# Linear attention and a max-out FFN on one core: first and last chunk by halves, one exponential over two PSUM banks, a new order

## Chip, cores, metric

The kernel runs on one core of one Trainium2 chip. The metric is the device time of one execution in microseconds; the kernel before took 294.62 us (median of three runs).

## What is computed

```python
def phi(x):                                   # x: q or k, (8, 8, 576, 64)
    proj = einsum('bhsd,df->bhsf', x, w_phi)  # 128 features
    proj = proj - max(abs(proj), axis=-1)
    return concatenate([exp(proj), exp(-proj)], axis=-1)
q_p, k_p = phi(q), phi(k)
kv  = einsum('bhsf,bhsd->bhfd', k_p, v);  z = sum(k_p, axis=2)
num = einsum('bhsf,bhfd->bhsd', q_p, kv); den = einsum('bhsf,bhf->bhs', q_p, z) + 1e-06
x   = (num / den) as (8 * 576, 512)           # 4608 tokens
h   = maximum(maximum(x @ w1, x @ w2), x @ w3)   # w1, w2, w3: 512 x 768
out = h @ w_out                               # 768 x 512
```

## The kernel before

Attention goes in 16 units: a unit is half a batch, four heads of 576 tokens. The 512 first tokens of each head are 16 tiles of 128 (four a head), the 64 tokens left of each two heads share a tile, so a unit has 18 tiles. `HU`, `MT` and `UT` are 4, 16 and 18.

The steps of a unit, by their names in the code: loads of q, k and v (`L`, `Lt` for the 64 tokens at the end of each head, `Lv`); for the units 0 to 3 q and k are loaded and cast by POOL's queue and transposed on PE (`T`, line 495) and copied (`Tc`), for the others they are cast (`C`, line 510) and transposed by a DMA. Then the projections of tokens on the rows (`G`, line 536) into `psq` and `psk`, the exponentials `ek` (line 545) and the absolute maxima `rk` and `rq` (line 548). The maxima of k scale v (`va`, line 566), and `K` (line 587) adds up kv and z. A second product, of transposed q (`M`, line 607), gives the features on the rows: `psm`, whose exponentials `eq` (line 613) go to `Eq`. `N` (line 638) multiplies them with kv for each of the two signs; `xu` scales the one by exp of minus twice the maximum (`sq`), `xw` adds the other, `xr` takes the reciprocal of the denominator and `x` (line 648) divides. The result is turned into `xT`: on PE for the units below `X_PE` = 6 (line 658, copied at 661), by a DMA transpose for the others (line 665).

The FFN goes in nine chunks: chunk b takes the 512 first tokens of each head of batch b, the last chunk the 8 x 64 tokens left over (`c_i == B`). The maximum with w1 is taken out of the products: w2 - w1 and w3 - w1 (`wd`, line 763) go through a product each (`up`, `up2`, line 688), are cut at zero and maximised (`t1`, line 696 or 698; `h`, line 694), and x @ (w1 @ w_out) is added to the down product (lines 716 and 721). The products `wt` and `wm` (lines 775 and 789) make w1 @ w_out once. `osb` (line 729) copies a result out of PSUM, `store` writes it.

The weights are loaded by four DMAs of POOL's queue (line 421).

The order of the work is written out by hand: the string `PLAN` lists every step once, with the step's number, the engine (T is PE, D DVE, A ACT, G POOL, S the SP queue), the buffer slots that it takes, and a due time. Each engine runs its steps in the order of the list and waits for what a step needs; the due time sets nothing else but where idle products could be put between, and there are none. PSUM's eight banks are slots as well. `4G0@0.4` is step 4 on POOL with slot 0.

The start of the list, with what the steps are: 4 and 5 load unit 0's q, 6 and 8 its k, 2 loads w_phi, 10 the ends of q (`Lt`), 11 v, 93 and 92 unit 1's k and q, 253 and 252 unit 3's, 177 and 176 unit 2's, 12 and 96 cast the ends of q for the units 0 and 1 (line 487), 1173 to 1176 load the weights:

```
4G0@0.4 6S0@0.4 2S@1.0 0G@1.2 5G@1.8 8S@2.2 93G1@2.7 10S0@2.8 92G@3.5 7D@3.7 11S0@4.1 3D@4.2 13T0@4.3 253G2@4.3
14D0@5.0 252G@5.2 9A@5.3 24T001200@5.8 19T34@6.0 27D@6.3 21A@6.5 12G@6.6 15T5@6.7 96G@6.8 23D@6.9 26A@7.0 17T6@7.2
178S0@7.2 16D@7.5 20A@7.5 177G0@7.5 25A@8.0 18D@8.1 29T70@8.2 22D@8.3 176G@8.4 39T35@8.5 63T6200@8.6 30A@8.7 28D@8.9
65A@9.2 1173G@9.2 94D@9.5 42D@9.6 34T41@9.7 31A@9.7 95S@9.8 33D@10.0 1176G@10.0 41A@10.2 36A@10.5 43D@10.6 101T7@10.7
```

13, 15 and 17 are unit 0's transposes on PE (17 those of the tail), 24, 19, 29, 34 and 39 its projections.

Of the kernel before, what the change touches and what calls it, by code (L numbers as in the profile page):

```python
# [19 lines left out]
P = 128  # L20
# [5 lines left out]
HU = 4  # L26
# [10 lines left out]
EARLY = 2  # L37
WARM = 28.0
# [8 lines left out]
class Buf:  # L47


    def __init__(self, pool, make):  # L50
        self.pool, self.make = pool, make
        self.users, self.tile, self.index, self.left, self.free = [], None, None, 0, 0.0
        self.locked = 0.0
# [31 lines left out]
4G0@0.4 6S0@0.4 2S@1.0 0G@1.2 5G@1.8 8S@2.2 93G1@2.7 10S0@2.8 92G@3.5 7D@3.7 11S0@4.1 3D@4.2 13T0@4.3 253G2@4.3  # L85
14D0@5.0 252G@5.2 9A@5.3 24T001200@5.8 19T34@6.0 27D@6.3 21A@6.5 12G@6.6 15T5@6.7 96G@6.8 23D@6.9 26A@7.0 17T6@7.2
178S0@7.2 16D@7.5 20A@7.5 177G0@7.5 25A@8.0 18D@8.1 29T70@8.2 22D@8.3 176G@8.4 39T35@8.5 63T6200@8.6 30A@8.7 28D@8.9
65A@9.2 1173G@9.2 94D@9.5 42D@9.6 34T41@9.7 31A@9.7 95S@9.8 33D@10.0 1176G@10.0 41A@10.2 36A@10.5 43D@10.6 101T7@10.7
1174G@10.8 32D@10.9 40A@10.9 99T3@11.1 64A@11.2 97T5@11.5 102D1@11.5 1175G@11.6 67A@11.7 37D@11.7 68T0@12.1 58T67@12.2
401S0@12.2 44A0@12.2 98D@12.3 66A@12.4 46G0@12.5 69A@12.9 100D@13.0 108T112511@13.1 35A@13.2 38D@13.6 62A@13.6  # L90
113T31@13.8 256G@13.9 181G@14.1 70A@14.1 112D@14.2 45G@14.3 48A@14.4 103T40@14.6 109A@14.6 117D@14.8 257T2@14.9
104A@15.1 111D@15.4 261T3@15.6 61A@15.6 329S0@15.6 47G@15.7 49G@15.9 262D2@16.0 105A@16.1 107D@16.2 52T073@16.4
59A@16.5 106D@16.8 110A@17.0 50G@17.2 116D@17.4 60A@17.5 118T45@17.7 259T0@18.0 53A@18.0 122D@18.1 128A1@18.2
114A@18.4 123T67@18.5 51G@18.6 121D@18.7 400S@18.8 130G1@18.8 54A@18.9 152T411@18.9 115A@19.1 126D@19.4 154A@19.6
127D@19.7 55T31@19.7 124A@19.9 260D@20.0 119A@20.1 129G@20.1 182T6@20.4 56A@20.6 258D@20.7 125A@20.8 186T0@20.9
71A0@21.1 147T37@21.3 187D0@21.3 132A@21.3 57D@21.5 153A@21.5 72T20@21.6 135G@21.7 183D@21.7 120A@21.8 131G@21.9
75T14@22.0 133G@22.2 149A@22.3 73D0@22.3 184T5@22.4 76D@22.8 155A1@22.8 328S@22.9 151A@23.0 136T162@23.0 74D@23.2
148A@23.4 134G@23.5 77D@23.6 83T10@23.7 150A@23.9 138D@24.0 142T34@24.2 185D@24.2 137A@24.4 80T27@24.6 145A@24.6
78D0@24.8 139T65@25.0 84D1@25.1 143A@25.1 79G0@25.2 81D@25.5 146A@25.6 1187T1@25.7 85D@25.9 327S@26.0 144A@26.1
1185T2@26.3 82D@26.3 1188A0@26.6 406G1@26.6 141D@26.7 159T40@26.9 140D@27.0 86D1@27.2 156T37@27.2 160D0@27.5  # L100
1186A@27.5 87G@27.5 1183T5@27.6 157D@27.9 164T61@28.2 161D@28.3 1184A@28.5 223T4300@28.6 158D@28.7 88T2@28.9 404G@29.0
165D1@29.2 90T0@29.2 225A@29.4 403G@29.5 179D1@29.6 167T75@29.6 166D@29.7 1195T6@29.9 89A@29.9 405G@30.1 254D@30.1
168D@30.2 227A@30.5 162D0@30.7 334G2@30.7 91D@30.9 255S@31.0 224A@31.0 1189T21@31.2 163D1@31.4 226A@31.5 1196A@32.0
169D@32.1 1D@32.5 206T007000@32.6 197T4365@32.7 170D1@32.7 1190A@32.8 209D@33.0 172T1@33.3 171D@33.3 208A@33.5
1191T2@33.6 207A@33.9 201D@34.0 198A@34.2 180S@34.2 1179G@34.6 210D@34.7 199A@34.8 174T0@34.9 205D@35.0 1193T4@35.2
203A@35.3 200D@35.6 175A@35.8 173D@36.2 1192A@36.4 188T7630@36.6 1178G@36.7 1194A@36.9 228T1@37.0 1207T2@37.2
195D@37.3 230A@37.4 189A@37.7 196D@37.9 1209T4@38.1 229A@38.2 1208A1@38.4 204D@38.5 407G@38.8 1205T1@39.0 191D@39.1
202A@39.3 1177G@39.5 408S1@39.6 1181D@39.7 194A@39.7 1203T3@39.9 1210A@40.2 192D@40.3 1215T2@40.7 211A0@40.7
# [184 lines left out]
def kernel(  # L293
# [95 lines left out]
    def side(t):  # L389
        return int(t >= MT // 2)  # L390
# [465 lines left out]
```

## Time and profile before

| | |
|---|---|
| three runs | 292.95, 296.05, 294.62 us; median 294.62 |
| the profiled execution | 292.23 us, of which the span from the first to the last instruction is 290.1 |
| mean granted TensorE clock | 0.994 |
| busy share of the span | PE 93%, PEld 52%, DVE 79%, ACT 71%, POOL 54% |
| chain that ended last | PE 74%, DMA 15%, DVE 6% |
| DMA | 49.92 MB in 70662 packets |

The profile's rows name a line, an engine, an operation and its tiles (written <- read), and give the start, the busy time, and in brackets the idle time just before with what ended it. Matmul records overlap in a pipeline, so PE's busy time holds short waits too. `POOLq` and `SPq` are rows of the engines' queues, which issue DMAs.

### The profile page before, as it was taken

The numbers are of one execution on the slowest core, as the hardware profiler recorded it, in microseconds if no ns is written. First come the engines' busy times: TensorE is split into PE (matmuls) and PEld (weight loads), VectorE is DVE, ScalarE is ACT, GpSimd is POOL, SyncE is SP. The second block draws the span as 40 slices with busy tenths as digits, with TensorE's granted clock in tenths as the row PEclk, the third lists the DMA queues.
The fourth block names the chain that finished last, engine by engine and source line by source line (L and its number), as shares of the span: only waits on it lengthen the run. The fifth ranks groups of instructions, "written<-read, shape, count | busy, mean of one in ns | idle before, by whom it ended". The sixth has DMA issues, their size and how long they took to land.

```text
span 290.1 us, 8572 instructions
## 1 busy us (share of the span) xinstructions
PE 270.6 (93%) x3502; PEld 151.3 (52%) x3502; DVE 230.2 (79%) x458; ACT 204.7 (71%) x493; POOL 157.7 (54%) x163
## 2 busy tenths in 40 slices
PE   1589997899999999998999999999999999999994
PEld 1367643456546645663565445655465555444442
DVE  2699886989998889998999988999999785264430
ACT  2699985789998899689864899999969681210001
POOL 7397659557678636576866396660758533100000
PEclk9998999999999999999999999999999999999999
DMA  7999998793897962799987899627084212100065
GB/s 141 226 280 215 262 259 198 207 273 119 299 279 158 244 192 46 182 321 282 254 245 198 209 333 206 127 21 217 5 129 139 90 37 62 66 3 2 0 217 145
DMA packets 70662, 49.92 MB, mean 172 GB/s; under 512 B 47072, under 2 KB 58720, under 8 KB 70624
## 3 DMA queue, kind: packets, MB, share of 16 engines
q1 hardware_dynamic: 65232, 44.25, 58.7%
q0 software_dynamic: 5312, 5.08, 10.7%
q8 instruction: 27, 0.44, 0.6%
q14 instruction: 11, 0.09, 0.1%
q10 hardware_dynamic: 80, 0.07, 0.1%
HBM read 34.67 MB, written 9.44 MB: 152 GB/s over the span
## 4 chain that ended last, share of the span: by engine, by line
PE 74%; DMA 15%; DVE 6%; issue 1%; POOL 1%; SPq 1%; DVEq 0%; POOLq 0%
PE ups L688 31%; PE ops L721 14%; DMA w_bf<-in_moe_w_dram 11%; PE ops L716 10%; PE psn L638 6%; PE kvps L587 5%; PE psq L536 4%; PE psm L607 3%; DMA q_raw<-in_q_dram 2%; DMA xT<-x_sb 2%; DVE w_bf L763 1%; DVE x_sb L648 1%; DVE y L644 1%; PE pxT L658 1%; PE psk L536 1%
## 5 line engine op out<-in xcount | busy, mean ns | idle before, releaser
L688 PE MATMUL ups<-xT,w_bf 128*128 128x512 bf16 x432 | 99.5, 379 | 4.2 <-DVE w_bf L763 1.4
L545 ACT ACTIVATE Ek<-psk 128x512 bf16<-128x512 f32 (+1 forms) x160 | 83.6, 572 | 12.9 <-PE psk L536 6.7
L566 POOL TENSOR_TENSOR vab<-v_raw,em 128x1152 bf16<-128x1152 f32 (+1 forms) x36 | 69.5, 1950 | 35.8 <-ACT em L558 35.8
L613 ACT ACTIVATE Eq<-psm 128x512 bf16<-128x512 f32 (+1 forms) x160 | 81.9, 588 | 3.1 <-PE psm L607 1.9
L688 PEld LDWEIGHTS <-w_bf 128*128 128x128 bf16 x432 | 39.9, 98 | 52.6 <-issue 4.4
L548 DVE TENSOR_REDUCE mk<-psk 128x4 f32<-128x512 f32 (+1 forms) x80 | 48.7, 630 | 4.7 <-PE psk L536 3.2
L721 PE MATMUL ops<-wout_bf,hT 128*128 128x512 bf16 (+1 forms) x222 | 51.7, 373 | 0.0
L548 DVE TENSOR_REDUCE mq<-psq 128x4 f32<-128x512 f32 (+1 forms) x80 | 48.6, 628 | 2.3 <-PE psk L536 1.3
L696 ACT ACTIVATE hT<-ups 128x512 bf16<-128x512 f32 x36 | 21.8, 611 | 29.0 <-PE ups L688 28.8
L694 DVE TENSOR_TENSOR hT<-hT,ups 128x512 bf16<-128x512 bf16 x54 | 35.2, 678 | 8.3 <-PE ups L688 7.5
L648 POOL TENSOR_TENSOR x_sb<-y,rden 128x640 bf16<-128x640 f32 x22 | 27.4, 1253 | 21.9 <-DVE rden L646 21.0
L641 DVE TENSOR_TENSOR y<-psn,sq 128x325 f32<-128x325 f32 x64 | 29.5, 488 | 6.9 <-PE psn L638 5.0
L721 PEld LDWEIGHTS <-hT 128*128 128x128 bf16 x222 | 20.5, 98 | 21.9 <-issue 0.5
L644 DVE TENSOR_TENSOR y<-y,psn 128x325 f32<-128x325 f32 x64 | 29.4, 488 | 1.4
L638 PEld LDWEIGHTS <-Eq 128*128 128x128 bf16 x640 | 25.0, 97 | 10.3 <-issue 2.5
L729 ACT COPY osb<-ops 128x512 f32<-128x512 f32 (+1 forms) x23 | 13.2, 583 | 23.0 <-PE ops L721 22.7
L638 PE MATMUL psn<-kv_sb,Eq 128*128 128x65 bf16 x640 | 27.5, 194 | 1.3 <-issue 0.4
L536 PE MATMUL psq<-wph,qkT 64*128 64x128 bf16 x288 | 25.9, 224 | 1.2 <-DVE qkT L500 1.0
L536 PEld LDWEIGHTS <-qkT 64*128 64x128 bf16 x576 | 18.6, 97 | 15.8 <-issue 12.0
L536 PE MATMUL psk<-wph,qkT 64*128 64x128 bf16 x288 | 25.4, 224 | 0.3 <-DVE v_raw L479 0.3
L716 PE MATMUL ops<-xT 128*128 128x512 bf16 x96 | 24.6, 380 | 0.0
L587 PE MATMUL kvps<-vab,Ek 64*128 64x65 bf16 x1152 | 22.7, 193 | 0.3 <-ACT Eq L613 0.2
(58 smaller groups left out, 259.9 us busy)
## 6 DMA issues: line engine op xcount, KB each, us to landing
v_raw<-in_v_dram SPq DMA_DIRECT2D x16, 576.0 KB, 7.2
out_dram<-osb SPq DMA_DIRECT2D x32, 256.0 KB, 3.4
k_raw<-in_k_dram SPq DMA_DIRECT2D x12, 576.0 KB, 5.4
q_raw<-in_q_dram SPq DMA_DIRECT2D x12, 512.0 KB, 5.5
w_bf<-in_moe_w_dram POOLq DMA_DIRECT2D x3, 768.0 KB, 25.1
q_raw<-in_q_dram SPq DMA_DIRECT2D x16, 64.0 KB, 5.5
qk_bf<-in_k_dram POOLq DMA_DIRECT2D x3, 288.0 KB, 7.3
qk_bf<-in_q_dram POOLq DMA_DIRECT2D x3, 256.0 KB, 9.9
```

What stands on the lines that cost most here:

```text
L536: nc.tensor.matmul(ps()[:, i, :], lhsT=cols[r0:r0 + D, :], rhs=wph[r0:r0 + D, :], start=True, stop=True)
L545: "ek", {"ACT": 0.485 if n == 4 else 0.28}, lambda s=s, t0=t0, n=n, psk=psk: nc.scalar.activation(Ek[s]()[:, t0:t0 + n, :], psk()[:, 0:n, ...
L548: reds.append(nd(kind, {"DVE": 0.607 if n == 4 else 0.34}, lambda ps=ps, m=m, t0=t0, n=n: nc.vector.tensor_reduce(m()[:, t0:t0 + n], ps()[ ...
L566: made.append(any_of(n_, lambda n_, g=g, t0=t0, t1=t1: (nc.vector if n_.eng == "DVE" else nc.gpsimd).tensor_tensor(vab()[:, g, t0:t1, 0:D] ...
L587: nc.tensor.matmul(kvps[ab]()[:, pr, g, :], lhsT=Ek[g]()[r, t, :], rhs=vab()[r, g, t, :], start=(pr == prs[0] and g + j == 0), stop=(pr == ...
L613: "eq", {"ACT": 0.485 if n == 4 else 0.28}, lambda s=s, t0=t0, n=n, psm=psm: nc.scalar.activation(Eq[s]()[:, t0 * P:(t0 + n) * P], psm()[: ...
L638: nc.tensor.matmul(psn[g]()[:, c, :], lhsT=Eq[g]()[:, t0:t0 + P], rhs=kv()[:, pr, ab, g, :], start=True, stop=True)
L644: sums.append(nd("xw", {"DVE": 0.42}, lambda ab=ab, psn=psn, y=y: nc.vector.tensor_tensor(y()[:, ab], y()[:, ab], psn[1](), ALU.add), [n_] ...
L688: nc.tensor.matmul(ups(), lhsT=w_bf[i + 1][:, ct, j * P:(j + 1) * P], rhs=tokens_of(ct), start=(ct == 0), stop=(ct == CT - 1))
L694: nc.vector.tensor_tensor(hT()[:, j, :], hT()[:, j, :], ups(), ALU.max)
L716: nc.tensor.matmul(ops_()[:, 0:width], lhsT=tile_of(ct, tt), rhs=line_w[c_i > MOVE][:, ct, cols], start=(ct == 0), stop=False)
L721: nc.tensor.matmul(ops_()[:, 0:width], lhsT=hT()[:, j, tt * P:(tt + 1) * P], rhs=wout_bf[:, j, cols], start=False, stop=(j == JT - 1))
```

## The change

- A unit's q tiles are put in another order (`tile_of_q`): first the two first tiles of each of the four heads, then the two second ones. So the product `M` and the exponentials of one step give the first 256 tokens of all four heads, and `N`, `xu`, `xw`, `xr`, `x` and the turning of x go by halves of the tokens (2 tiles, then 3 with the shared tile) where they went by pairs of heads.
- The two `M` products of a step write one tile of two PSUM banks, and one exponential of 1024 columns reads it, where there were two of 512.
- `xu` can run on ACT, as one small multiplication for each head and tile; 26 of the 64 do.
- The units 14 and 15 turn x on PE, as the first six do. For the units 0, 1, 14 and 15 the reciprocal is taken for each pair of heads.
- The chunks 0 and 7 go as two of 256 tokens each, the last one as 384 and 128.
- PSUM is one tile of eight banks, of which each buffer is a slice.
- Unit 0's second transposes need both loads of k; q's casts of the units 4 to 15 are in two pieces each.
- The list is rewritten as a whole. Its start, where 1155 to 1158 are the weights now, 251 and 250 load unit 3's k and q, and the steps 0 to 43 are what they were:

```
8S0@0.7 5G0@1.2 6S@1.3 2S@1.9 4G@2.1 92G1@2.9 10S0@3.1 0G@3.8 9A@3.9 93G@4.3 11S0@4.4 176G2@5.2 7D@5.4 3D@5.9 177G@6.0
15T0@6.0 13T1@6.7 16D0@6.7 1155G@6.8 14D@7.4 29T000200@7.5 1158G@7.7 34T34@7.7 30A@8.0 33D@8.0 24T15@8.1 19T67@8.4
36A@8.4 1156G@8.4 32D@8.6 20A@8.9 38D@9.2 1157G@9.2 35A@9.4 23D@9.8 21A@9.9 12G@10.1 25A@10.4 37D@10.4 17T0@10.4
251G0@10.8 31A@10.9 18D@11.0 28D@11.2 26A@11.3 64T000@11.4 58T2@11.5 96G@11.7 39T46@11.7 65A@11.8 22D@11.8 59A@12.1
```

The last of unit 3's loads is `250G@29.9`; its transposes stand at 41.2 to 43.6, among the products of chunk 0, where the list before had them at 14.9 to 18.0.

The core of the diff, without the list:

```diff
+SOON = (0, 1, 14, 15)
+SPLIT = (0, 7)
...
+    banks = psum.tile([P, 8, SM], FP32, name="banks")
...
+    def tile_of_q(t):
+        pr, half, ab, c = t // 8, t // 4 % 2, t // 2 % 2, t % 2
+        return 8 * pr + 4 * ab + 2 * half + c if t < MT else t
...
-            psms = [bank("psm", [P, 4 * P]) for _ in parts]
+            if len(parts) == 2:
+                psm = Buf(slots.setdefault("bank", Slots(8)), lambda b: banks[:, b.index:b.index + 2, :], 2)
+                psms = [(lambda psm=psm, i=i: psm()[:, i, :]) for i in range(2)]
...
-            for (t0, n), psm in zip(parts, psms):
-                for s in range(2):
-                    eqs.setdefault(t0, []).append(nd(
-                        "eq", {"ACT": 0.485 if n == 4 else 0.28}, lambda s=s, t0=t0, n=n, psm=psm: nc.scalar.activation(
-                            Eq[s]()[:, t0 * P:(t0 + n) * P], psm()[:, 0:n * P], EXP, scale=1.0 - 2.0 * s), [a], [psm, Eq[s]], locks=[psm]))
+            for s in range(2):
+                def to(s=s, parts=parts):
+                    if len(parts) == 1:
+                        return Eq[s]()[:, MT * P:UT * P]
+                    c0 = parts[0][0] * P
+                    return Eq[s]()[:, 0:MT * P].rearrange("p (i c) -> p i c", i=2)[:, :, c0:c0 + SM]
+                n_ = nd("eq", {"ACT": 0.905 if len(parts) == 2 else 0.265}, lambda s=s, psm=psm, to=to: nc.scalar.activation(
+                    to(), psm(), EXP, scale=1.0 - 2.0 * s), [a], [psm, Eq[s]], locks=[psm])
...
+        for half in range(2):
+            nt = 2 + half
...
+                a = nd("N", {"PE": 0.13 * nt + 0.01}, nmm, n_kvs[pr] + eqs[8 * pr + 4 * half] + (eqs[MT] if half else []),
+                       Eq + [kv] + psn)
+                n_ = nd("xu", {"DVE": 0.07 + 0.14 * nt, "ACT": 0.22 * nt}, None, [a, n_sq], [psn[0], sq, y], locks=[psn[0]])
...
+                    for ab in range(2):
+                        for c in range(nt):
+                            nc.scalar.mul(y()[:, pr, ab, c, :], psn[0]()[:, ab, c, :], sq()[:, pr, half, ab, c:c + 1])
...
-        if u < X_PE:
...
+            if u < X_PE or u in SOON:
+                pxT = bank("pxT", [P, 2, nt, P], BF16)
...
-        chunk(b, units[2 * b]["done"] + units[2 * b + 1]["done"], lambda ct, b=b: xT[:, b, ct, 0:SM],
+        for c0, n in ([(0, 256), (256, 256)] if b in SPLIT else [(0, SM)]):
+            ready = [x for u in (2 * b, 2 * b + 1) for half in range(2) if 256 * half < c0 + n and c0 < 256 * half + 256
+                     for x in units[u]["done"][half]]
...
+    for b0, b1 in ((0, 6), (6, 8)):
+        chunk(B, lasts[b0:b1], b0 * ST, (b1 - b0) * ST, lambda ct, b0=b0, b1=b1: xT[:, b0:b1, ct, SM:SM + ST],
```

More of the change, by code (lines that the diff above doesn't have):

```diff
@@ L274, in fill @@
             if b.pool is pool and b is not spare:
-                x = spans.setdefault(id(b), [b.index, n.start, n.end])
-                x[1], x[2] = min(x[1], n.start), max(x[2], n.end)
+                for i in range(b.width):
+                    x = spans.setdefault((id(b), i), [b.index + i, n.start, n.end])
+                    x[1], x[2] = min(x[1], n.start), max(x[2], n.end)
     for n in order:
@@ L651, in attention @@
[L651 to L663 removed]
+        divs, done = [], []
@@ L664, in xdma @@
+        if not done:
             def xdma():
@@ L822, in fn @@
         def fn():
[L823 to L824 removed]
+            nc.tensor.matmul(banks[:, i, :], lhsT=idle, rhs=idle.unsqueeze(1).to_broadcast([P, 4, P]), start=True, stop=True)
         return fn
```

489 lines of the change are left out of this document (261 added, 228 removed).

## The prediction

> **What bounds the kernel now.** I read the page first, then busy time in stretches of 20 us, then the timeline of the start.
>
> ```profile
> span 290.1 us, 8572 instructions
> PE 270.6 (93%) x3502; PEld 151.3 (52%) x3502; DVE 230.2 (79%) x458; ACT 204.7 (71%) x493; POOL 157.7 (54%) x163
> ```
> ```profile
> 0.00:20.00 20.00, 10.36 (x157) 7.26 (x157) 11.00 (x22) 11.33 (x26) 13.37 (x26) 1.00 1.02 210
> 20.00:40.00 20.00, 18.97 (x382) 13.77 (x381) 18.57 (x48) 19.13 (x48) 12.39 (x16) 0.91 1.16 242
> 40.00:60.00 20.00, 16.73 (x188) 8.01 (x186) 16.75 (x27) 14.73 (x34) 14.38 (x10) 1.00 0.85 212
> ...
> 100.00:120.00 20.00, 20.00 (x246) 10.76 (x244) 18.12 (x33) 19.38 (x49) 9.44 (x9) 1.00 0.52 140
> 120.00:140.00 20.00, 19.09 (x254) 10.24 (x253) 18.09 (x39) 16.40 (x40) 15.23 (x15) 1.00 1.11 276
> 140.00:160.00 20.00, 19.88 (x328) 11.74 (x327) 19.04 (x40) 12.95 (x37) 14.05 (x16) 1.00 0.88 237
> ...
> 180.00:200.00 20.00, 19.39 (x344) 11.64 (x340) 19.26 (x43) 18.71 (x45) 9.86 (x8) 1.00 0.59 121
> ...
> 240.00:286.00 46.00, 46.00 (x235) 21.85 (x231) 19.30 (x32) 6.57 (x12) 3.38 (x5) 1.00 0.23 66
> ```
>
> The columns are PE, PEld, DVE, ACT, POOL, then the granted clock, the DMA share and GB/s. From 60 us to the last product at 286 us PE is never idle for long: 0.91, 0.12 and 0.61 us in three stretches, 1.64 us together. So the end is (PE's work) plus (PE's idle time), and nearly all idle time lies ahead of 60 us: 9.64 us before 20, 1.03 before 40, 3.27 between 40 and 60. Anything that shortens DVE, ACT or POOL after 60 us pays only if it removes a piece of those 1.64 us, or a wait so short that overlapping matmul records hide it. The start is where to look.
>
> ```profile
> 5.28 1.06 PE L495 MATMUL tps<-ident,qk_bf 128*64 128x128 bf16 x16 [5.28 <-DMA qk_bf<-in_q_dram]
> 11.38 0.42 PE L495 MATMUL tps<-ident,qk_bf 128*64 128x128 bf16 x4 [2.22 <-POOL qk_bf L487]
> 42.79 1.90 PE L688 MATMUL ups<-xT,w_bf 128*128 128x512 bf16 x8 [0.71 <-POOL w_bf L763]
> 44.87 1.90 PE L688 MATMUL ups<-xT,w_bf 128*128 128x512 bf16 x8 [0.18 <-POOL w_bf L763]
> 48.16 1.90 PE L688 MATMUL ups<-xT,w_bf 128*128 128x512 bf16 x8 [1.39 <-DVE w_bf L763]
> 52.85 2.38 PE L688 MATMUL ups<-xT,w_bf 128*128 128x512 bf16 x10 [0.90 <-DVE mq L548]
> ```
> ```profile
> 11.85 0.29 DVE L500 COPY qkT<-tps 128x256 bf16<-128x256 bf16 x1 [1.95 <-PE tps L495]
> 47.05 1.05 DVE L763 TENSOR_TENSOR w_bf<-w_bf 128x1024 bf16<-128x1024 bf16 x1 [2.52 <-DMA w_bf<-in_moe_w_dram]
> ```
> ```profile
> 12.42 0.60 ACT L545 ACTIVATE Ek<-psk 128x512 bf16<-128x512 f32 x1 [2.12 <-PE psk L536]
> ```
> ```profile
> 11.04 0.53 POOL L487 CAST qk_bf<-q_raw 128x128 bf16<-128x128 f32 x2 [4.63 <-DMA q_raw<-in_q_dram]
> ...
> 13.88 0.76 POOL L421 DMA_DIRECT2D w_bf<-in_moe_w_dram x1
> ```
>
> Two things hold the start. First, the tail of q (64 rows a head) lands at 11.04. PE's list has the transposes of that tail ahead of the later projections, so PE waits 2.22, DVE 1.95 and ACT 2.12 us. Second, POOL stands 4.63 us at the cast of the same tail, and the weight loads are behind it in POOL's list: they are issued only from 13.88. The third weight releases DVE at 47.05, and PE idles on weight differences (L763) at 42.79, 44.87 and 48.16.
>
> **The change part by part.**
>
> *The tail's transposes moved back.* The new list gives unit 0 four projection steps (29, 34, 24, 19) before the tail's transposes (17); the old list had two.
>
> ```profile
> 7.79 0.69 DVE L548 TENSOR_REDUCE mk<-psk 128x4 f32<-128x512 f32 x1 [0.70 <-PE psk L536]
> 8.39 0.68 DVE L548 TENSOR_REDUCE mq<-psq 128x4 f32<-128x512 f32 x1
> ```
> ```profile
> 8.24 2.06 ACT L545 ACTIVATE Ek<-psk 128x512 bf16<-128x512 f32 x4 [0.56 <-PE psk L536]
> ```
>
> A step hands DVE two reductions, 0.60 us start to start, and ACT two exponentials at 2.06/4 = 0.52. Four steps are 4.8 us of DVE's and 4.1 us of ACT's work from about 8 us on, which covers the time to 11.85 and 12.42. DVE and ACT set the pace of the attention units up to 40 us (18.57 and 19.13 of 20), so those units come 2.0 us earlier. Bounds: nothing, if something else is late (the second half of k, or w_phi, which is now issued behind both k loads), and 2.12.
>
> *The weight loads moved ahead of the tail's cast and of unit 3's loads.* POOL's list now runs six loads and the identity, then the four weights, and only then the tail's cast. POOL still reaches that cast before its data.
>
> ```profile
> L421 POOL DMA_DIRECT2D w_bf<-in_moe_w_dram x3: 760/787/792, 13.9 to 16.2; - x3
> ...
> DMA to landing us min/median/max: 14.2/25.1/30.8
> ```
> ```profile
> w_bf<-in_moe_w_dram POOLq DMA_DIRECT2D x3, 768.0 KB, 25.1
> ...
> qk_bf<-in_k_dram POOLq DMA_DIRECT2D x3, 288.0 KB, 7.3
> qk_bf<-in_q_dram POOLq DMA_DIRECT2D x3, 256.0 KB, 9.9
> ```
>
> The first w_bf landed at 13.9 + 14.2 = 28.1, the third at 16.2 + 30.8 = 47.0. With wout_bf between them that is three times 768 KB in 18.9 us, 6.3 us each, 122 KB/us. They queue rather than run side by side, so the issue itself is not the price; the bytes ahead are. Unit 3's q and k, 288 + 256 = 544 KB, go from ahead of the weights to behind them: 544/122 = 4.5 us earlier, 42.5 instead of 47.0. With attention 2.0 us earlier the weights gain 2.5 us on it. Of PE's 3.27 us of waits between 40 and 60 that removes 2.5.
>
> What is late next is unit 3. Its transposes ran in PE's idle time at the start; now they stand among the first chunk's products. They are 36 matmuls.
>
> ```profile
> 24.75 0.81 PE L495 MATMUL tps<-ident,qk_bf 128*64 128x128 bf16 x20
> ```
>
> Twenty of them took 0.81 us here, so 36 take 1.5, and 2.4 at the start's 1.06/16; the records of a group end with one product's latency, so I take 1.1 us. They fill the 0.8 us of weight waits that are left, but the idle time that they used to fill comes back at the start. Start together: -2.0 (attention) - 3.27 (waits gone or filled) + 1.1 = **-4.2 us**. Bounds: 0 if the weights land no earlier, since then attention's 2.0 turns into a longer weight wait; and -5.4 if the transposes too find idle time.
>
> *Units 14 and 15 turn x on PE.* 20 more transposes and 4 more copies, two DMA transposes fewer.
>
> ```profile
> 72.36 0.28 PE pxT L658 x5
> ...
> 282.93 0.86 PE ops L716 x4
> ...
> 285.08 0.44 PE ops L716 x4
> ```
>
> 0.28/5 = 0.056 each: **+1.1 us** of PE work. What it buys is chunk 7 being ready earlier, and in 240:286 PE has no idle time to give back. Bounds 1.0 and 1.2.
>
> *Chunks 0 and 7 by halves; the last chunk as 384 and 128.* Four matmuls 256 wide take 0.44 against 0.86 for 512, so halving costs nothing. The 48 of 128 columns go at the transposes' 0.056 against 0.86/16 = 0.054: **+0.1 us**. The end after the last product is unchanged.
>
> *psn by halves of the tokens, ACT for part of the scaling.* Still 40 psn matmuls a unit, 0 us on PE.
>
> ```profile
> L613 ACT ACTIVATE Eq<-psm 128x512 bf16<-128x512 f32 x128 | 71.2, 634 | 2.3 <-PE psm L607 1.7
> L613 ACT ACTIVATE Eq<-psm 128x256 bf16<-128x256 f32 x32 | 12.4, 404 | 0.8 <-PE psk L536 0.3 <-PE psm L607 0.2
> L558 ACT ACTIVATE em<-mk 128x18 f32<-128x18 f32 x28 | 4.7, 222 | 2.0 <-DVE mk L548 1.9
> L641 DVE TENSOR_TENSOR y<-psn,sq 128x325 f32<-128x325 f32 x64 | 29.5, 488 | 6.9 <-PE psn L638 5.0 <-ACT em L558 0.9 <-DVE x_sb L648 0.5
> L694 DVE TENSOR_TENSOR hT<-hT,ups 128x512 bf16<-128x512 bf16 x54 | 35.2, 678 | 8.3 <-PE ups L688 7.5 <-ACT hT L696 0.8
> ```
> ```profile
> 18.57 0.33 ACT L558 ACTIVATE em<-mk 128x9 f32<-128x9 f32 x2
> ```
>
> From 256 to 512 columns an exponential grows by 230 ns, so 174 ns are fixed. 64 merged pairs save 64 x 0.174 = 11 us of ACT's records, less where back-to-back ones overlap. Against that, the list puts 26 of the 64 scalings (xu) on ACT: 134 small multiplications. Two small ACT operations took 0.33 us, one alone 0.222, so a second adds 0.11: 15 us, 30 us without overlap. DVE loses 26 of its 488 ns products and gains 28 evacuations' fixed part (678 at 512, 488 at 325: 0.16 each). ACT ends near 205 to 224 of 290 us, DVE lower than now; neither becomes the mean bound, so 0 on PE's path. The cover is the other queued products; without it ACT's surplus is the price, which is a rival below.
>
> *More, smaller POOL work* (q's casts by halves, x in four pieces a unit) has 132 us of idle POOL over it: 0, and unit 15's x pieces if that cover fails, under 1 us.
>
> *The new order after 60 us.* The largest of the three waits is one row:
>
> ```profile
> 136.61 1.67 PE L688 MATMUL ups<-xT,w_bf 128*128 128x512 bf16 x7 [0.89 <-DMA xT<-x_sb]
> ```
>
> Such waits hang on the exact order, which is rewritten. Bounds -1.64 and +2 (as many waits again); I take -0.6, since half a unit's psn no longer needs all its exponentials.
>
> **Sum**: -4.2 + 1.1 + 0.1 - 0.6 = **-3.6 us**. The profiled execution took 292.23 us, 2.13 outside its 290.1 span; so 286.5 of span, 288.6. It lies 2.39 under the median of the three runs, 294.62; against that median the forecast is **291.0 us**. Its own range adds up the bounds that are likely together: -6.6 to -2.0, 288.0 to 292.6.
>
> **Rivals.** *The start gains nothing*: the DMA share is already above 1 in 0:40, unit 3's loads only change places, and PE waits for unit 3's data instead of the weights. For it: those transposes stand in order in PE's list. Against: the bytes ahead of each weight do shrink. Time: 0 + 1.1 + 0.1 = +1.2, 295.8.
>
> *Slower: the scalings on ACT reach PE.* Place: 48 to 250 us, where ACT is busy up to 19.38 of 20. Without overlap a multiplication costs 0.222 rather than 0.11, 134 x 0.112 = 15 us more on ACT; DVE's sum, the psn banks and PE wait in list order behind it. If half reaches PE: +7.5 - 3.6 = +3.9, 298.5. It breaks even when 24% reaches PE and is slower by over 1% from 43% on. Against: only 26 steps, and ACT has some idle time after most. The Trainium skill, "ScalarE: Activation LUTs", under "What ACT_TABLE_LOAD costs", says that each per-partition pointer operand adds about 93 ns to an ACTIVATE; these multiplications scale by such an operand and no row here shows one. By it the surplus would be 134 x 0.093 = 12.5 us and the sum, with half of it on PE, +2.6, an estimate.
>
> *More than forecast*: the transposes of unit 3 find idle time (-5.4), all 1.64 us go, and short hidden waits go with DVE's relief: -6 to -8, about 287.5.
>
> *That the merged exponential isn't one pass* would leave ACT 11 us higher, which PE doesn't see; no case of its own.
>
> **Numbers.** Forecast 0.50, nothing at the start 0.17, slower by ACT 0.16, more 0.17. About 1% (2.9 us) is what a measurement of this kernel tells from no change, so the marks are 291.7 and 297.6. Four fifths of the forecast's range lie under 291.7: 0.40 + 0.16 (nearly all of "more") = 0.56 faster; 0.10 + 0.16 = 0.26 same; 0.18 slower, the ACT case and the ends of the others. The range goes from 286.5 to 298.0.
>
> **What would show it.** Right: the weights' issues start before 9 us; the third w_bf frees DVE near 43; no wait of 2 us at the tail's transposes; PE idle in 40:60 under 1 us; the last product near 282 to 283. Wrong: PE waiting over 2 us on unit 3's q or k; the small ACT products at 0.2 us start to start with DVE's sums and then PE waiting on them; more than 3 us of PE idle time after 60 us.

## The result and the profile after

The changed kernel takes 301.61 us (median of 4 runs, 301.44 to 302.05) against 293.78 us (291.72 to 296.05) for the kernel before on the same chip: a ratio of **1.0296, 95% interval [1.0244, 1.0347]**, some 8 to 9 us slower. The ratios, here and below, and the times of e7 and g2, are of fast runs alone, since some runs come out over 1.5% above the fastest of their kernel: six of e7's twelve, two of g2's twelve, and a few of the kernel before. The forecast was 291.0 us, with a range up to 298.0. The case that came is the rival in which the scalings on ACT reach PE, and it came larger than I had priced it.

The page of the changed kernel: span, busy time by engine, and the shares of the chain that ended last.

```profile
span 299.7 us, 9122 instructions
...
PE 272.7 (91%) x3628; PEld 166.0 (55%) x3666; DVE 235.1 (78%) x486; ACT 229.0 (76%) x567; POOL 163.5 (55%) x215
...
PE 66%; DVE 15%; ACT 13%; issue 4%; DMA 2%; DVEq 0%; ACTq 0%; POOLq 0%
```

PE's work hardly grew (270.6 to 272.7, with 38 of its 3666 matmul records missing from this trace) and the span grew by 9.6 us, so PE waits. ACT rose from 204.7 to 229.0 and DVE from 230.2 to 235.1; both now stand on the chain, with 13% and 15%.

Busy time by stretch (length, then PE, PEld, DVE, ACT and POOL with their counts, granted clock, DMA share, GB/s), first before, then after:

```profile
60.00:100.00 40.00, 39.99 (x605) 23.52 (x604) 35.86 (x78) 35.72 (x90) 29.17 (x30) 1.00 0.86 229
```
```profile
0.00:20.00 20.00, 10.97 (x171) 8.21 (x173) 13.07 (x26) 13.11 (x28) 14.34 (x25) 1.00 1.07 200
20.00:40.00 20.00, 19.37 (x354) 13.80 (x351) 18.76 (x50) 19.26 (x43) 14.84 (x17) 1.00 1.16 258
40.00:60.00 20.00, 15.68 (x272) 12.15 (x270) 18.57 (x34) 15.25 (x49) 11.68 (x17) 1.00 0.51 140
60.00:100.00 40.00, 37.91 (x546) 21.80 (x551) 33.66 (x69) 36.73 (x94) 30.43 (x41) 1.00 0.83 210
100.00:140.00 40.00, 37.15 (x544) 21.32 (x548) 37.05 (x71) 36.36 (x92) 27.68 (x38) 1.00 0.89 233
140.00:180.00 40.00, 38.58 (x520) 21.63 (x520) 36.21 (x73) 35.80 (x79) 24.97 (x39) 1.00 0.91 211
180.00:220.00 40.00, 39.09 (x488) 21.73 (x495) 34.24 (x68) 35.33 (x97) 22.48 (x24) 1.00 0.71 143
220.00:260.00 40.00, 39.29 (x506) 22.04 (x505) 26.81 (x54) 27.30 (x69) 14.68 (x14) 1.00 0.25 64
```

Up to 40 us PE is busy 1.0 us more than before. In 40:60, where the forecast had it nearly without idle time, it is busy 15.68 against 16.73, so at 60 us nothing of the start's gain is left. From 60 to 260 us PE's idle time adds up to some 8.0 us (15 matmul records are missing there, so the figure is rough), where it was 1.6: a slow loss spread over all later stages, and well over the 3 us that I had named as a sign of being wrong.

Most of what I had named as signs of the start did appear. POOL's queue, and the weights' time from issue to landing:

```profile
6.31 0.79 POOL L444 DMA_DIRECT2D w_bf<-in_moe_w_dram  x1
7.06 0.86 POOL L444 DMA_DIRECT2D wout_bf<-in_moe_w_out_dram  x1
7.87 1.54 POOL L444 DMA_DIRECT2D w_bf<-in_moe_w_dram  x2
```
```profile
DMA to landing us min/median/max: 12.8/22.3/26.6
```

The weights are issued from 6.31 us, and the third lands about 8.6 + 26.6 = 35.2 us, earlier even than the 42.5 I forecast (47.0 before). No wait of PE is for a weight to land any more. What PE waits on in their place stands in its list between 39 and 50 us, from its first product of chunk 0 on:

```profile
39.77 1.47 PE L752 MATMUL banks<-xT,w_bf 128*128 128x256 bf16 x12
41.96 0.60 PE L752 MATMUL banks<-xT,w_bf 128*128 128x256 bf16 x4 [0.72 <-DVE hT L762]
44.02 0.51 PE L721 MATMUL banks<-ident,x_sb 128*128 128x128 bf16 x6 [1.46 <-DVE x_sb L711]
...
47.49 0.60 PE L752 MATMUL banks<-xT,w_bf 128*128 128x256 bf16 x4 [1.43 <-DVE hT L762]
```

All three are DVE; the last one holds a wait of the weight loads too, 1.4 us for DVE's difference of the weights (L827). DVE's list, and POOL's, in the same stretch:

```profile
39.76 1.81 DVE L711 TENSOR_TENSOR x_sb<-y,rden 128x384 bf16<-128x384 f32 x1
41.50 0.41 DVE L762 TENSOR_SCALAR hT<-banks 128x256 bf16<-128x256 f32 x1
41.83 2.13 DVE L711 TENSOR_TENSOR x_sb<-y,rden 128x384 bf16<-128x384 f32 x1
43.89 0.69 DVE L827 TENSOR_TENSOR w_bf<-w_bf 128x1024 bf16<-128x1024 bf16 x1
44.50 0.41 DVE L762 TENSOR_SCALAR hT<-banks 128x256 bf16<-128x256 f32 x1
44.84 2.27 DVE L827 TENSOR_TENSOR w_bf<-w_bf 128x1024 bf16<-128x1024 bf16 x1
...
47.89 0.67 DVE L827 TENSOR_TENSOR w_bf<-w_bf 128x1024 bf16<-128x1024 bf16 x1
```
```profile
34.87 6.28 POOL L827 TENSOR_TENSOR w_bf<-w_bf 128x1024 bf16<-128x1024 bf16 x3
41.11 2.44 POOL L600 TENSOR_TENSOR vab<-v_raw,em 128x1152 bf16<-128x1152 f32 x1
43.50 0.67 POOL L604 CAST vab<-em 128x36 bf16<-128x36 f32 x1
43.99 2.56 POOL L600 TENSOR_TENSOR vab<-v_raw,em 128x1152 bf16<-128x1152 f32 x1
```

Read the ends side by side (start plus time). DVE's long products end at 41.57, 43.96 and 47.11; POOL's that run beside them end at 41.15, 43.55 and 46.55. Each of the three finishes about half a microsecond after POOL's, whatever its size; the same difference of the weights takes 0.67 at 47.89, when POOL runs none, and 2.27 at 44.84. At 43.89 it takes 0.69: there it started just ahead of POOL's product of 43.99, which is the longer one (2.56 against 2.44), and POOL's small cast of 43.50 did not hold it. Between them DVE's evacuation of PSUM (L762, 0.41) is not stretched. So a DVE product with both operands in SBUF that starts behind a POOL product stands until that one is done. The Trainium skill, "SBUF — State Buffer", "Who interferes with whom", has this rule: a DVE instruction with two SBUF inputs and a GpSimd instruction that reads SBUF exclude each other, and the one that starts second waits for the whole of the other. These rows agree for a DVE product that starts second to a POOL product; the other order and the small cast they do not settle.

The other loss is on ACT: the small products of the scaling, as a group by form and twenty in a row.

```profile
L697 ACT ACTIVATE y<-banks,sq 128x65 f32<-128x65 f32 x134 | 30.1, 352 | 7.8 <-POOL x_sb L711 2.9 <-PE banks L684 2.8 <-DVE x_sb L711 1.4
```
```profile
53.89 4.22 ACT L697 ACTIVATE y<-banks,sq 128x65 f32<-128x65 f32 x20
```

Start to start they take (4.22 - 0.352)/19 = 0.204 us, not the 0.11 of my sum: 134 of them are 27.3 us of ACT.

### The profile page after: what moved, and what is told of

It reads as the page before. It is cut to its first block, busy times and chain, and to the rows that moved or that the text cites. A ratio compares the mean times of both kernels' runs of the same rounds, so it can differ in the third digit from the quotient of the medians.

```text
span 299.7 us, 9122 instructions
## 1 busy us (share of the span) xinstructions
PE 272.7 (91%) x3628; PEld 166.0 (55%) x3666; DVE 235.1 (78%) x486; ACT 229.0 (76%) x567; POOL 163.5 (55%) x215
## 4 chain that ended last, share of the span: by engine, by line
PE 66%; DVE 15%; ACT 13%; issue 4%; DMA 2%; DVEq 0%; ACTq 0%; POOLq 0%
PE banks L752 24%; PE banks L785 12%; PE banks L780 8%; ACT y L697 7%; PE banks L570 6%; PE banks L621 5%; DVE x_sb L711 4%; PE banks L684 3%; ACT Ek L579 3%; DVE y L699 3%; PE banks L646 2%; PE banks L518 2%; DVE mq L582 2%; DMA qk_bf<-in_q_dram 2%; PE banks L721 2%
## 5 line engine op out<-in xcount | busy, mean ns | idle before, releaser
L752 PE MATMUL banks<-xT,w_bf 128*128 128x512 bf16 (+3 forms) x562 | 102.5, 325 | 4.9 <-DVE hT L762 2.2
L579 ACT ACTIVATE Ek<-banks 128x512 bf16<-128x512 f32 (+1 forms) x160 | 83.5, 582 | 12.4 <-PE banks L570 7.6
L655 ACT ACTIVATE Eq<-banks 128x1024 bf16<-128x1024 f32 (+1 forms) x96 | 73.7, 841 | 5.8 <-PE banks L646 5.0
L711 POOL TENSOR_TENSOR x_sb<-y,rden 128x384 bf16<-128x384 f32 (+1 forms) x43 | 32.4, 768 | 47.1 <-DVE rden L705 42.1
L582 DVE TENSOR_REDUCE mk<-banks 128x4 f32<-128x512 f32 (+1 forms) x80 | 48.7, 626 | 5.0 <-ACT Ek L579 2.0
L785 PE MATMUL banks<-wout_bf,hT 128*128 128x512 bf16 (+1 forms) x215 | 51.3, 373 | 0.6 <-issue 0.3
L582 DVE TENSOR_REDUCE mq<-banks 128x4 f32<-128x512 f32 (+1 forms) x80 | 48.8, 626 | 1.1 <-PE banks L570 0.8
L758 DVE TENSOR_TENSOR hT<-hT,banks 128x512 bf16<-128x512 bf16 (+3 forms) x72 | 38.0, 547 | 9.7 <-PE banks L752 8.3
L699 DVE TENSOR_TENSOR y<-y,banks 128x260 f32<-128x260 f32 (+1 forms) x64 | 30.5, 490 | 10.8 <-ACT y L697 6.8
L697 ACT ACTIVATE y<-banks,sq 128x65 f32<-128x65 f32 x134 | 30.1, 352 | 7.8 <-POOL x_sb L711 2.9
```

The costliest lines, as they stand in the source:

```text
L579: "ek", {"ACT": 0.485 if n == 4 else 0.28}, lambda s=s, t0=t0, n=n, psk=psk: nc.scalar.activation(Ek[s]()[:, t0:t0 + n, :], psk()[:, 0:n, ...
L582: reds.append(nd(kind, {"DVE": 0.607 if n == 4 else 0.34}, lambda ps=ps, m=m, t0=t0, n=n: nc.vector.tensor_reduce(m()[:, t0:t0 + n], ps()[ ...
L655: n_ = nd("eq", {"ACT": 0.905 if len(parts) == 2 else 0.265}, lambda s=s, psm=psm, to=to: nc.scalar.activation(to(), psm(), EXP, scale=1.0 ...
L697: nc.scalar.mul(y()[:, pr, ab, c, :], psn[0]()[:, ab, c, :], sq()[:, pr, half, ab, c:c + 1])
L711: nc.vector if n_.eng == "DVE" else nc.gpsimd).tensor_tensor(
L752: nc.tensor.matmul(ups(), lhsT=w_bf[i + 1][:, ct, j * P:(j + 1) * P], rhs=tokens_of(ct), start=(ct == 0), stop=(ct == CT - 1))
```

## The experiments

Three theories stood at first. **Theory 1**: ACT's small products with their pointer operand are the loss. **Theory 2**: DVE's products behind POOL's are. **Theory 3**: halves and new order are the loss by themselves.

**e1_xu_dve.** In the list, 26 steps of kind xu get the letter of DVE.

```
-229A@49.0   (26 such)
+229D@49.0
```

> The changed kernel with all 64 scalings (xu) on DVE, same order of steps. Theory 1 (the 134 small ACT products cost 0.197 us start to start and PE waits for them down the list): the time falls by 3 to 6 us from 301.6, to a ratio of 1.010 to 1.020 to the kernel before. Theory 2 (x on DVE stands behind POOL's products): DVE gets 26 products of 0.36 or 0.50 us more, 11 us, and nothing gets better; ratio 1.03 to 1.05. Theory 3 (the halves and the new order by themselves): within 1% of the changed kernel, 1.025 to 1.035.

298.58 us, ratio 1.0192 [1.0127, 1.0258]. A third of the loss goes, with intervals that overlap a little. DVE rises from 235.1 to 243.2 us; that this is what bounds the gain was not tested.

**e2_xu_const.** The products stay on ACT but with a constant; the scaling is left out.

```
-nc.scalar.mul(y()[:, pr, ab, c, :], psn[0]()[:, ab, c, :], sq()[:, pr, half, ab, c:c + 1])
+nc.scalar.mul(y()[:, pr, ab, c, :], psn[0]()[:, ab, c, :], 1.0)
```

> The changed kernel with the same 134 products on ACT, but scaled by the constant 1.0 instead of a column of sq (this leaves out those scalings). By the Trainium skill's page on ScalarE the pointer operand is worth 0.093 us each: start to start falls from 0.197 to about 0.105, 12 us of ACT. Theory 1: PE gets a third to a half of it, 4 to 6 us, ratio 1.010 to 1.017. Theories 2 and 3: under 1 us, ratio 1.027 or more.

295.43 us, ratio **1.0084 [1.0054, 1.0114]**: 0.0212, or 6.2 us, lie in the pointer operand alone, a little more than theory 1 expected. The same group by form, and fourteen in a row:

```profile
L697 ACT ACTIVATE y<-banks 128x65 f32<-128x65 f32 x134 | 18.5, 251 | 8.4 <-PE banks L684 3.5 <-POOL x_sb L711 2.9 <-DVE x_sb L711 1.5
```
```profile
54.19 1.87 ACT L697 ACTIVATE y<-banks 128x65 f32<-128x65 f32 x14
```

352 - 251 = 101 ns of each record, and (1.87 - 0.251)/13 = 0.125 us start to start instead of 0.204. 134 x 0.079 = 10.6 us of ACT, which is what its total lost (229.0 to 218.4). So 6.2 of 10.6 us reached the end. The Trainium skill, "ScalarE: Activation LUTs", "What ACT_TABLE_LOAD costs", gives about 93 ns for a pointer operand; the records, 101 ns apart, come near it, while start to start the difference here is 79 ns.

**e3_x_pool** and **e4_both.** The 21 products of x that DVE does go to POOL, in the changed kernel and in e1.

```
-173D, 171D ... (21 of kind x)
+173G, 171G ...
```

> The changed kernel with all of x (64 pieces) on POOL, none on DVE. POOL gets 21 pieces of 0.56 or 0.77 us more. Theory 2: the 8.5 us that DVE's 21 pieces take over their undisturbed 0.43 and 0.55 us go, and 3 to 5 us of them were on PE's path: ratio 1.013 to 1.020. Theory 1 or 3: no gain, 1.025 to 1.035, or a loss where x on POOL is late behind vab (2.1 us each).

> The changed kernel with xu on DVE and x on POOL together. Theories 1 and 2 both, adding up: 6 to 9 us, ratio 0.999 to 1.010. Theory 3: the loss is in the halves and the order, ratio 1.02 or more.

303.01 us, 1.0343 [1.0284, 1.0402], and 300.68 us, 1.0253 [1.0191, 1.0315]: both above the same kernel without the move (1.0296 and 1.0192), with intervals that overlap, and neither shows the gain that theory 2 expected; 1.0253 is where theory 3 put e4. POOL is no refuge: a product of 384 columns takes it 0.86 us, DVE undisturbed 0.55, and PE's waits for x between 30 and 66 us are 3.4 us in e3 where they were 2.5. If theory 2 holds all the same, POOL's instructions have to get shorter, not DVE's fewer.

**e5_split.** e2 with the whole cut: POOL's products of v in pieces of 6 tiles, those of the weights' differences in single row blocks. The edit in short:

```
+for a0, a1 in [(x, min(x + 6, t1)) for x in range(t0, t1, 6)]: vab product of tiles a0:a1
+for ct in range(CT): w_bf[i + 1][:, ct, c] -= w_bf[0][:, ct, c]
```

> The changed kernel with its 134 small products scaled by 1.0 in place of the pointer operand (so x is not scaled by exp(-2 max) there), and POOL's products of v (18 or 9 tiles) and of the weights' differences cut into pieces of 6 tiles and of one row block. Beside the run with the constant alone (295.43 us, 1.0084). Theory 2, DVE's products of two operands in SBUF stand behind a POOL product of 2.4 us that runs beside them: the waits of PE for x (2.4 us) and for hT (2.3 us) between 40 and 65 us shrink to under 1 us each, and the time to 292.5 to 294 us, ratio 0.995 to 1.003. Theory 3, what is left is the halves and the new order themselves: 295 to 296.5 us, ratio 1.006 to 1.012.

290.89 us, ratio **0.9933 [0.9902, 0.9965]**: 0.0151 or 4.4 us from the cut against e2, and 0.7% faster than the kernel before. DVE's products of x, by form, before the cut (in e2) and behind it:

```profile
L711 DVE TENSOR_TENSOR x_sb<-y,rden 128x384 bf16<-128x384 f32 x9 | 11.5, 1285 | 0.1
L711 DVE TENSOR_TENSOR x_sb<-y,rden 128x256 bf16<-128x256 f32 x12 | 7.3, 612 | 0.1
```
```profile
L713 DVE TENSOR_TENSOR x_sb<-y,rden 128x384 bf16<-128x384 f32 x9 | 7.3, 820 | 0.1
L713 DVE TENSOR_TENSOR x_sb<-y,rden 128x256 bf16<-128x256 f32 x12 | 6.2, 515 | 0.1
```

The same 21 products take 13.5 us in place of 18.8. PE's waits for x and hT are gone from its list in that stretch (1.6 us for POOL's pieces of the differences stand there now), and PE has 78% of the chain, where it had 66%. The price is POOL's: its total rises from 163.8 to 175.3 us.

With both remedies no loss is left. But e5 leaves the scaling out, so this does not yet clear the halves and the new order (theory 3); f4 below, which leaves nothing out, bears on them.

**e6_before_act.** The kernel before, 26 scalings by ACT.

```
+for c in range(5):
+    nc.scalar.mul(y()[:, ab, c, :], psn[0]()[:, c, :], sq()[:, 2 * pr + ab, c:c + 1])
```

> The kernel before, with 26 of its 64 scalings of 128x325 (the units of the changed kernel's 26 steps) done by ACT as five small products with a pointer operand each, 130 in all; nothing else. Theory 1, the small products alone are the loss: ACT 130 x 0.197 = 25.6 us more, DVE 26 x 0.488 = 12.7 us less, and the time 297 to 301 us, ratio 1.012 to 1.028. Rival, they cost only in the new order with its halves: 292 to 295 us, ratio 0.997 to 1.006.

309.42 us, ratio **1.0561 [1.0510, 1.0611]**, twice the upper end of what I expected. The page of this kernel (ACT's total rose by 25.6 us), with the shares of its chain:

```profile
PE 274.1 (89%) x3461; PEld 153.0 (50%) x3502; DVE 221.8 (72%) x432; ACT 230.3 (75%) x623; POOL 158.5 (52%) x163
...
PE 50%; ACT 25%; DMA 14%; DVE 5%; issue 2%; POOL 1%; SPq 1%; POOLq 0%; ACTq 0%; DVEq 0%
```
```profile
60.00:100.00 40.00, 35.65 (x462) 19.68 (x466) 28.55 (x55) 37.17 (x110) 25.39 (x25) 1.00 0.74 200
```

Some 16 of the 25.6 us reach the end, although DVE lost 8.4 us of work. In 60:100 PE falls from 39.99 to 35.65, with ACT at 37.17 of 40. So the move of this work is slow in the old order too, and it is not the new order that makes it dear.

**e7_start.** The kernel before with the start of the changed one. The list in short:

```
 POOL: 4 0 5 93 92 [177 176 1173 1176 1174 1175] 12 96 [253 252] ...
 PE:   17T behind 34T; unit 2's transposes in unit 3's place, unit 3's near 40 us
```

> The kernel before with the start of the changed one alone: the four weights' loads ahead of the casts of q's tail and of unit 3's loads (unit 3 takes unit 2's place and the other way round in the transposes), the tail's transposes behind the products of the first two groups, unit 3's transposes near 40 us; nothing after 48 us moved. Theory A, as predicted for the start: 4.2 us less, 288.5 to 291 us, ratio 0.980 to 0.992, third weight landed near 36 us and no PE wait for weights. Theory B, the gain is there at 35 us and goes between 38 and 55 us into DVE's differences of the weights behind POOL's products and into unit 3's late data: 292 to 295 us, ratio 0.995 to 1.005.

293.5 us, ratio 1.0032 [0.9993, 1.0071]: not faster. My list had a fault of its own: in its trace PE waits 1.66 us at 21.89 for the cast of unit 2's tail, which stands too late on POOL. So the start was run again, mended, in e11 and g2.

**e8_exp_two.** The changed kernel, each exponential of 1024 columns as two of 512.

```
-nc.scalar.activation(to(), psm(), EXP, ...)
+for i in range(2): nc.scalar.activation(to()[:, i], psm()[:, i], EXP, ...)
```

> The changed kernel with each exponential of 1024 columns done as two of 512 from the same two-bank tile; nothing else. If the merging saves what back-to-back instructions show (2 x 0.478 - 0.904 = 0.05 us each, 3.3 us of ACT in all): 301.5 to 303.5 us, ratio to before 1.028 to 1.036. If it saves the fixed part that I predicted (0.174 us each, 11 us of ACT): 305 us or more, ratio over 1.04.

303.22 us, ratio 1.0349 [1.0304, 1.0393], 0.0053 above the changed kernel, with intervals that overlap. The same four steps on ACT, first in the changed kernel, then here:

```profile
78.68 3.83 ACT L655 ACTIVATE Eq<-banks 128x1024 bf16<-128x1024 f32 x4
```
```profile
78.74 4.08 ACT L655 ACTIVATE Eq<-banks 128x512 bf16<-128x512 f32 x8
```

0.25 us for four merged pairs, 0.06 each: 64 save 4 us of ACT (its total differs by 3.6), not the 11 us that I took from the records of single ones.

**e9_split_ptr, e10_before_split, e11_start_split, e12_dve_split.** Three of these hold less than their expectations say: in e9, e10 and e12 only the differences were cut, and v's products were left whole; in e9 and e12 the exponentials stood in two as well. e11 has the whole cut, of v too. So e9 is read against e8, and e11 against f2 below, not against e10.

```
+for ct in range(CT): w_bf[i + 1][:, ct, c] -= w_bf[0][:, ct, c]
```

> The changed kernel with POOL's products of v and of the weights' differences cut into pieces of 6 tiles and of one row block; the small products on ACT keep their pointer operand, so nothing is left out. Theories 1 and 2 as separate losses: the cut is worth what it was worth with the constant (1.0084 to 0.9933, 0.015, 4.4 us), ratio 1.010 to 1.018, 295.5 to 298 us. Rival, the two losses overlap (ACT is late anyway, so DVE's delay is not what PE waits for): ratio 1.022 to 1.030.

> The kernel before with the same cut of POOL's products, nothing else. Theory 2: before has 10 products of x on DVE and the weights' differences, 10.4 and 3.5 us with some 3 us of waiting for POOL in them, and PE waits 2.3 us for differences between 40 and 60 us, so 1 to 3 us less: 289.5 to 291.5 us, ratio 0.990 to 0.997. Rival, the stall is one that only the changed order puts on PE's path: ratio 0.998 to 1.004.

> The kernel before with the cut and with the start of the changed one, this time with unit 2's casts of q's tail ahead of unit 3's k and its tail's transposes left behind, since in the first such run PE had 2.3 us more idle time between 20 and 30 us from POOL's late casts. Theory A (the start is worth 3 to 4 us once POOL no longer holds DVE): 2.5 to 4 us under the cut alone, ratio 0.977 to 0.987. Theory B (unit 3's data come as much later as the weights come sooner): within 1 us of the cut alone or slower, ratio 0.990 to 1.000.

> The changed kernel with all 64 scalings on DVE (1.0192 alone) and the cut; nothing left out. If the cut is worth 0.015 here too: ratio 1.001 to 1.008, 293 to 295 us. If DVE, with 14 us more work, is the bound by itself: 1.012 to 1.020. If the pointer products are the whole of the rest, it comes to the level of the constant with the cut: 0.991 to 0.996.

e9: 300.96 us, 1.0273 [1.0237, 1.0309], against e8's 1.0349: the differences' cut is worth 0.0076 in the changed order, with intervals that just overlap. e10: 294.69 us, 1.0063 [1.0031, 1.0094]: in the old order the same cut costs, which neither expectation had. PE's longest wait between 35 and 60 us is there 2.0 us for DVE's maxima (`mq`), where the wait for them was 0.9 us before; that this is the whole cost was not tested. e11: 294.18 us, 1.0039 [1.0017, 1.0060]: against f2's 1.0004 the mended start is 0.0035 the wrong way, with intervals that overlap, and not the 2.5 to 4 us of gain that theory A expected. e12: 296.44 us, 1.0127 [1.0090, 1.0164], 0.0065 under e1, with intervals that overlap too.

**f1_split_ptr, f2_before_split, f4_dve_split.** The whole cut, as in e5, in the changed kernel with its pointers, in the kernel before, and in e1.

> The changed kernel with POOL's products of v cut into pieces of 6 tiles and those of the weights' differences into single row blocks (the whole cut; the run called e9_split_ptr had the differences' cut alone, with the exponentials in two); pointer operands kept, nothing left out. If the two losses are separate, the whole cut is worth 0.015 here as with the constant: ratio 1.010 to 1.019. If ACT is late anyway: 1.022 to 1.030.

> The kernel before with the whole cut. The cut of the differences alone made it slower by 0.0063. Theory 2: cutting the products of v frees its 10 products of x on DVE (10.4 us, 0.23 us each over the undisturbed 0.81) and gives 0.003 to 0.008 back: ratio 0.997 to 1.004. Rival, nothing on PE's path waits there: 1.005 to 1.012.

> The changed kernel with all 64 scalings on DVE (1.0192 alone) and the whole cut; nothing left out. If the cut is worth 0.015 here: ratio 1.001 to 1.008. If DVE's 243 us are the bound by then: 1.012 to 1.020.

f1: 298.53 us, **1.0204 [1.0169, 1.0239]**: the cut is worth 0.0092 with the pointers, 0.0151 without them. That lies between the two expectations: the two losses overlap in part, as far as the intervals tell. Put the other way round, f1 and e5 differ in the pointer alone, and that is 0.0271, 7.9 us.

f2: 292.85 us, 1.0004 [0.9980, 1.0027]: the kernel before has nothing to gain from the whole cut. f4: 296.65 us, 1.0137 [1.0103, 1.0170]: with all scalings on DVE the cut does not reach the level of before. f4's page:

```profile
PE 272.4 (92%) x3628; PEld 166.0 (56%) x3666; DVE 238.8 (81%) x512; ACT 202.8 (69%) x433; POOL 174.6 (59%) x288
```

f2 is its partner: the whole cut, all scalings on DVE, nothing left out, the old order. The 0.0133 between them, 3.9 us, is in neither ACT's small products nor POOL's long ones, so it lies in the rest of the change, the halves and the new list with its start above all. DVE has 238.8 us in 512 instructions where f2 has 230.2 in 458; ACT has about the same (202.8, 204.9). That these 8.6 us of DVE are the cause was not tested, and the list was written for ACT to do 26 of the scalings. So theory 3 is not ruled out.

**f3_pool_scale.** f1, with a step's scaling as one evacuation on ACT and one product on POOL; the edit in short:

```
+nc.scalar.mul(y()[:, pr, :, 0:nt, :], psn[0]()[:, :, 0:nt, :], 1.0)
+nc.gpsimd.tensor_tensor(y()[:, pr, :, 0:nt, :], y()[:, pr, :, 0:nt, :], sq broadcast, ALU.mult)
```

> The changed kernel with the whole cut, and its 26 steps on ACT done as one evacuation of 128x260 or 128x390 by ACT with a constant, and one product with the scale on POOL; nothing left out. ACT has 26 instructions in place of 134, about 11 us less than with the pointer and some 5 us less than with the small constant ones; POOL 26 x 0.7 = 18 us more. If ACT's time is what reached PE: ratio 0.985 to 0.997. Rival, the longer chain (ACT, POOL, then DVE's sum) and POOL's list give it back: 1.00 to 1.02.

304.03 us, 1.0380 [1.0348, 1.0412]: the rival's way, and beyond its 1.02. ACT's total falls to 213.3 us, and it is slower all the same:

```profile
L698 POOL TENSOR_TENSOR y<-y,sq 128x390 f32<-128x390 f32 x15 | 12.6, 837 | 13.6 <-ACT y L697 13.6
```

POOL stands 13.6 us waiting for ACT's evacuations, with its list of v and x queued behind, and has 20% of the chain where it had 6% in f1. A step more in the chain costs more here than ACT's time.

**g1_before_vcut and g2_start_vcut.** The kernel before with v's cut alone, and the same with the mended start.

> The kernel before with POOL's products of v cut into pieces of 6 tiles, the differences left whole. If the two cuts add up (whole cut 1.0004, the differences' cut alone 1.0063): ratio 0.991 to 0.997. Rival, on the kernel before neither does anything and the two runs differed by chance: 0.998 to 1.004.

> The same with the changed kernel's start (weights' loads ahead of unit 3's, the tail's transposes late, unit 3's transposes near 40 us). Theory A, the start is worth the forecast 4.2 us: 0.010 or more under the run with the cut of v alone. Theory B, it gives back what it gains (with the differences' cut the pair stood at 1.0063 and 1.0039): within 0.004 of the run with the cut of v alone.

g1: 292.71 us, **0.9965 [0.9939, 0.9992]**, as expected if the two cuts' effects add up; g2: 293.2 us, 1.0007 [0.9977, 1.0038]. The start gains nothing here: 0.0042 the wrong way, after 0.0035 the wrong way in e11, and e7 stands at 1.0032. Each of the three is within its intervals of no effect; none is near the forecast gain of 0.014. PE's waits up to 60 us, g1 first, then g2 (us, times, longest):

```profile
PE tps L496 <- POOL qk_bf L488: 1.4, 1, 1.4
PE ups L690 <- DVE w_bf L765: 1.4, 1, 1.4
PE pm L791 <- DMA wout_bf<-in_moe_w_out_dram: 1.2, 1, 1.2
PE ups L690 <- POOL w_bf L765: 1.0, 2, 0.8
PE psq L537 <- DVE qkT L501: 0.8, 1, 0.8
```
```profile
PE psq L536 <- DVE qkT L500: 2.0, 3, 0.8
PE kvps L588 <- POOL vab L571: 1.9, 1, 1.9
PE ups L689 <- POOL w_bf L764: 1.0, 2, 0.8
PE tps L495 <- DVE qkT L500: 0.9, 1, 0.9
```

The waits for the tail, for wout_bf and for DVE's differences go (1.4 + 1.2 + 1.4 = 4.0 us), and waits for POOL's v and DVE's copies of qkT come (1.9 + 1.2 + 0.9 = 4.0 us).

g1 is the only version with nothing left out that came below the kernel before, by 1 us, and its interval ends just under 1. No version of the changed kernel that keeps the scaling did.

## Why the prediction was wrong, point by point

**psn halves, ACT for part of the scaling: the step that failed.** It said 15 us for the small products, 11 us saved by the merged exponentials, and "0 on PE's path". Measured: 27.3 us and some 4 us. ACT rose by 24.3 us to 229.0, not by 4, and above the 205 to 224 that I had for it. The price of a second product, 0.11 us, came from two operations of 9 columns without a pointer operand; at 65 columns it is 0.125 with a constant and 0.204 with a pointer. And the cover that I named, "the other queued products", does not exist: of the pointer's part alone 6.2 us (e2) to 7.9 us (f1 against e5) reach the end, and of the whole move in the old order 16 us (e6). Taking the scalings back to DVE gains less in the changed order, 3.0 us (e1) or 2.0 us (f4 against f1), since DVE then has 8 to 9 us more to do and the rest of the loss stays. A mean of 71% busy was read as room, in stretches where ACT had 35.7 of 40. The rival for this case had the mechanism, the place and a price near the measured one (0.222 us against 0.204 for a multiplication); its time, 298.5 us, stayed short of 301.61, and its error was the chance I gave it. The 7 us that merging did not save, of the kind "which PE doesn't see" in my text, left ACT still less room; merging as a whole is worth 0.0053 (e8), within the intervals.

**The start, -4.2 us: sized wrong.** Most signs came (weights early, no wait for their landing, the wait for the tail shorter), and the gain did not. The tail's wait shrank from 2.22 to 1.57 us only (PE at 11.87), because the copy of its transposes stands behind DVE's maxima; PE is 0.6 us ahead at 20 us, where I had 2.0. The third weight came 11.8 us earlier, 7.6 of them from the earlier issue, which I had said was not the price; it bought nothing at 60 us. In the changed kernel three DVE products behind POOL's take 3.6 us of PE between 41 and 48 us, and PE's idle time in 40:60 is 4.3 us, not under 1. In the old order the waits move to v and qkT (g1, g2). I had removed waits one at a time and not asked what DVE, busy 18.6 us of 20 here, and POOL's list would be late with next.

**"More, smaller POOL work: 0".** What the added instructions cost by themselves was not tested; the length of POOL's products was not harmless. That DVE's products of x and differences of the weights would stand behind POOL's 2.4 us just where PE waits for them was in no rival. It is worth 2.7 us (f1) to 4.4 us (e5).

**Units 14 and 15, halves, the new order.** With both losses out, the changed order stands 0.0071 under the kernel before with the same cut (e5 0.9933, f2 1.0004), about 2 us, where my sum had 3.6; but e5 leaves the scaling out. With everything done and the scalings on DVE in both, it stands 0.0133 above (f4, f2), 3.9 us. How this divides among the halves, the units 14 and 15 and the list was not measured. My sum had DVE lower than before; its total is 235.1 us in the changed kernel and 238.8 in f4, where it was 230.2.

The low end of the forecast's range does not follow from its bounds: -5.4 + 1.0 + 0.1 - 1.64 is -5.9, not -6.6. Nothing else rests on it.

## What to carry to other kernels

A product moved to another engine is priced by a row of the same form, pointer operand included, taken start to start; where no such row exists, the whole of it is put on the path as soon as that engine is about nine tenths busy in the stretch. Two engines that read SBUF are costed as a pair: a DVE product that PE waits for wants short POOL products beside it, and a cut that helps in one order can cost in another (0.0076 gained, 0.0063 lost). A start that removes three waits is worth only what the next engine in line is early by.

## What the runs showed of the hardware

- A pointer operand on ACT: 0.204 against 0.125 us start to start at 65 columns.
- Merging two exponentials of 512 columns across two banks: 0.06 us, although single records suggest 0.17.
- A DVE product with two SBUF operands that starts beside a running POOL product: 1.81 to 2.27 us, ending 0.4 to 0.6 us after POOL's; undisturbed 0.55 (128x384) and 0.67 us (128x1024).
- The cut of POOL's products: three differences of 2.12 us became twelve pieces of 0.80 us, 9.1 us in place of 6.3.
